# Loading a, q and k from SyncE's queue in single rows, in turn with crossbar transposes, in a fused linear-attention and MLP kernel

## Chip, cores, metric

One core of a Trainium2 chip. The metric is the device time in microseconds (us) of one execution; lower is better. Medians below are over all executions of a kernel.

## The reference

A gated linear recurrence per head, then a two-layer MLP with GELU on its output (shapes: 4 batches, 8 heads, 768 steps, head size 48; MLP 384 to 2048 to 384).

```python
for t in range(S):
    state = alpha[:, :, t, :, None] * state + np.einsum('bhd,bhe->bhde', k[:, :, t], v[:, :, t])
    y[:, :, t] = np.einsum('bhd,bhde->bhe', q[:, :, t], state)
# x = y as [3072, 384]
h = x @ w_in
g = 0.5 * h * (1.0 + np.tanh(c * (h + 0.044715 * h * h * h)))
return g @ w_out
```

## The kernel before

The steps are cut into 6 chunks of 128 and the batches into 2 halves, which gives 12 "pairs" (chunk, half). For each pair: load a (alpha), q, k, v; la = ln a; cum = running sum of la on TensorE; b = exp(cum), binv = exp(-cum), bend; q' = q b and k' = k binv (`qp`, `kp`); q' and k' transposed (`qkT`); scores `at` on TensorE; mask; `yps`; copied to x; x transposed (`xT`). Block m of the MLP is layer 1 (`hT`, GELU to `gT`) and layer 2 (`acc`) of pair m. A small planner in the kernel orders all instructions of all engines ahead of time, from planned costs `W`; engines then execute that order.

```python
DECAYS = {-1: (0, 1), 1: (2, 3), 2: (4,), 3: (5,), 4: (6, 7), 5: (8,), 6: (9,), 7: (10,), 8: (11,)}
TURN_QK, TURN_X = (8, 9, 10, 11), (8, 9, 10, 11)      # pairs transposed by the DMA crossbar
BUFS = dict(ca=1, yk=2, ff=4, la=3, qp=4, kp=4, b8=2, qkT=4, atm=6, x=3, ot=6, bend=8, a=4, q=4, k=4, v=6)
...
def load(self, n, c, i, lo=0, hi=2):
    def emit(e):
        ...
        src = self.src[n][2 * i + lo:2 * i + hi].rearrange("b h s d -> s (b h) d")[c * C:(c + 1) * C]
        (nc.sync if e == "SP" else nc.gpsimd).dma_start(u[n][:, lo:hi].rearrange("t b h d -> t (b h) d"), src)
...
def turn_dma(self, u, n):                               # crossbar transpose of q' or k'
    self.nc.sync.dma_start_transpose(self.qkT(u)[:, "qk".index(n)]..., u[n + "p"]...)
...
# GELUs of block m wait for the exponentials of DECAYS[m - 1];
# the logarithms of DECAYS[m] wait for the last GELU of block m
g = s.add("gelu", ..., [t] + between[m - 1] + ...)
ln.deps.append(gs[m][-1])
```

`DECAYS` sets the lead: the pairs in DECAYS[m] get their decays between the GELUs of blocks m and m + 1.

Of the kernel before, what the change touches and what calls it, by code (L numbers as in the profile page):

```python
# [5 lines left out]
BF16 = mybir.dt.bfloat16  # L6
F16 = mybir.dt.float16
F32 = mybir.dt.float32
# [3 lines left out]
LN_EXP, GELU = 6, 0  # L12


W = dict(
    ln=760, exp=720, bend=170, gelu4=510, gelu2=340, table=1290,
    cum=530, t8=450, t4=225, attn=340, kv=170, inter=170, intra=205, tx=168, l1_4=655, l1_2=340, l2=655,
    qk2=910, qk1=500, ev8=650, ev4=350, mask=640, st=1400, st0=700, xc=520, xe=330, ot=540,
    ev8_act=960, ev4_act=520, xc_act=450, xe_act=450, ot_act=450,
    strip=2120, cast=1500, weight=1850, dma=2100, issue=1100, wissue=760, sp=100, store=2600, turn=1250, landed=2200, xbar_qk=1500, xbar_x=1000, first=3470, cold=500, fill=216, zero=1100,  # L20
)
LAT = {"SP": 0, "PE": 210, "ACT": 110, "DVE": 90, "POOL": 0}

# [1 line left out]
class Task:  # L25


    def __init__(self, kind, cost, prio, emit, deps=(), table=None, land=None, stream=None, xbar=0, late=0):
        self.kind, self.cost, self.prio, self.emit = kind, cost, prio, emit
        self.deps, self.takes = list(deps), []  # L30
        self.table, self.land, self.stream, self.xbar = table, land, stream, xbar
        self.late = late
        self.end = self.done = None

    def take(self, tag, *users):
# [4 lines left out]
class Scheduler:  # L40
# [9 lines left out]
    def order(self):  # L50
        free = {e: 0 for e in LAT}
        taken = {tag: [] for tag in self.bufs}
        table, wire, xbar, head, out = LN_EXP, 0, 0, 0, []
        left = {e: sorted((t for t in self.tasks if e in t.cost), key=lambda t: t.prio) for e in LAT}

        def given(tag):

            n, at = len(taken[tag]) - self.bufs[tag], 0
            for u in taken[tag][n] if n >= 0 else ():
                if u.done is None:  # L60
                    return None
                at = max(at, u.done)
            return at

        def ready(t):
            if t.stream not in (None, head):
                return None
            at = 0
            for d in t.deps:
                if d.done is None:  # L70
                    return None
                at = max(at, d.done)
            for tag, _ in t.takes:
                g = given(tag)
                if g is None:
                    return None
                at = max(at, g)
            return at

        def put(t, at, e):  # L80
            nonlocal wire, xbar
            for tag, users in t.takes:
                taken[tag].append(users)
            t.start, t.end, t.engine, t.load = at, at + t.cost[e], e, None
            free[e] = t.end
            t.done = t.end + LAT[e]
            if t.land is not None:
                wire = t.done = max(wire, t.end + W["dma"] - t.land) + t.land
            if t.kind in ("turn", "store"):
                xbar = t.done = max(xbar, t.end + W["landed"] - t.xbar) + t.xbar  # L90
                t.done += t.late
            out.append(t)

        while any(left.values()):
            best = None
            for e in LAT:
                found = []
                for t in left[e]:
                    at = ready(t)
                    if at is not None:  # L100
                        turn = W["table"] if t.table not in (None, table) else 0
                        at = max(at, free[e] + turn)
                        found.append((at, t, at - turn))
                if found:
                    window = min(f[2] for f in found) + 60
                    at, t, _ = min((f for f in found if f[2] <= window), key=lambda f: (f[1].prio, f[0]))
                    if best is None or at < best[0]:
                        best = at, e, t
            assert best is not None, "no task can go on"
            at, e, t = best  # L110
            if e == "PE" and self.fill and at < self.until and at - free[e] > 500:
                g = given("ff")
                n = int((at - max(free[e], g if g is not None else at) - 100) * 0.8 // W["fill"])
                if not free[e]:
                    n = int((at - W["zero"]) // W["cold"])
                if n > 0:
                    f = Task("fill", {"PE": n * W["fill"]}, 0, self.fill(n))
                    put(f.take("ff", f), max(free[e], g), e)
            put(t, at, e)
            if t.stream is not None:  # L120
                head += 1
            if t.table not in (None, table):
                table = t.load = t.table
            for q in t.cost:
                left[q].remove(t)
        return out
# [9 lines left out]
class _Kernel:  # L136
# [6 lines left out]
    LOADS = ("0", "1", "in 0", "in 1", "in 2", "in 3", "out 0", "out 1", "out 2", "out 3",  # L143
             "2", "3", "4", "5", "6", "7", "8", "9", "10", "11")

    TURN_QK, TURN_X = (8, 9, 10, 11), (8, 9, 10, 11)
    BUFS = dict(ca=1, yk=2, ff=4, la=3, qp=4, kp=4, b8=2, qkT=4, atm=6, x=3, ot=6, bend=8,
                a=4, q=4, k=4, v=6)

# [63 lines left out]
    def load(self, n, c, i, lo=0, hi=2):  # L213

        nc, C, H, D = self.nc, self.C, self.H, self.D
        u = self.p[c, i]

        def emit(e):
            if n not in u:
                u[n] = self.tile(n, [C, 2, H, D], BF16 if n == "v" else F32)  # L220
            src = self.src[n][2 * i + lo:2 * i + hi].rearrange("b h s d -> s (b h) d")[c * C:(c + 1) * C]
            (nc.sync if e == "SP" else nc.gpsimd).dma_start(u[n][:, lo:hi].rearrange("t b h d -> t (b h) d"), src)  # L222
        return emit

    def load_w(self, which, part):
# [203 lines left out]
    def tasks(self):  # L429
        s = self.s = Scheduler(self.BUFS, self.fill, 60000)  # L430
# [3 lines left out]
        pairs = list(self.p)  # L434


        loads, n = {}, 0

        def load(key, cost, emit):
            nonlocal n  # L440
            land = W[{"v": "cast", "w": "weight"}.get(key[0], "strip")]
            loads[key] = s.add("load", {"POOL": cost}, n, emit, land=land // 2 if key[0] != "w" and key[1] in self.SPLIT else land)
            n += 1

        def rows(m, names="aqkv"):
            for lo, hi in self.parts(m):
                for r in names:
                    load((r, m, lo), W["issue"] * (hi - lo) // 2, self.load(r, *pairs[m], lo, hi))
                    loads[r, m, hi - 1] = loads[r, m, lo]
# [6 lines left out]
        for step in self.LOADS:  # L456
            if step == "0":
                rows(0, "qkv")
            elif step.isdigit():
                rows(int(step))  # L460
            else:
                weights(*step.split())


        states, ys, xts, lns, ends = {}, {}, {}, {}, {}
        for m, (c, i) in enumerate(pairs):
            u, P = self.p[c, i], 100 * m
# [3 lines left out]
            for lo, hi in self.parts(m):  # L471
                n = hi - lo
# [10 lines left out]
                step = 1 if early else n  # L483
# [7 lines left out]
            exps[0].take("b8", *qp, *kp)  # L491
            vs, kvs, tq, cs, users = [], [], [], [], []
            if m in self.TURN_QK:
                tq = [s.add("turn", {"SP": W["turn"]}, P + 10, self.turn_dma(u, n), d, xbar=W["xbar_qk"]) for n, d in (("q", qp), ("k", kp))]
                owner, turned = tq[0], tq
            for j in range(2):
                b, o = 2 * i + j, P + 10 + 3 * j
                k = kp[j]
# [18 lines left out]
                          ms + turned + [loads["v", m, j]] + ([states[b, c - 1]] if c else []))  # L517
                xc = s.add("x", {"ACT": W["xc_act"], "DVE": W["xc"]}, P + 20 + j, self.x(u, j), [y])
                if m in self.TURN_X:
                    xe = tx = s.add("turn", {"SP": W["turn"]}, P + 22 + j, self.turn_x_dma(u, j, c, b), [xc], xbar=W["xbar_x"])  # L520
                else:
                    tx = s.add("tx", {"PE": W["tx"]}, P + 22 + j, self.turn_x(u, j), [xc])
                    xe = s.add("xe", {"DVE": W["xe"]}, P + 22 + j, self.turned_x(u, j, c, b), [tx])
                    tx.take("yk", xe)
# [4 lines left out]
                xts[c, b], ys[b, c] = xe, y  # L529
                vs.append(y)  # L530
                if c < NCH - 1:
                    kv = s.add("kv", {"PE": W["kv"]}, P + 30 + j, self.kv(u, j), [k, loads["v", m, j]])
                    st = states[b, c] = s.add("st", {"DVE": W["st" if c else "st0"]}, P + 30 + j, self.carry(u, j, c, b),
                                              [kv, be[j]] + ([states[b, c - 1], ys[b, c - 1]] if c else []))
                    kv.take("yk", st)
                    vs.append(kv)
                    kvs.append(kv)
                    cs.append(st)
# [106 lines left out]
```

## Time and profile before

| | before |
|---|---|
| time, median | 188.67 us (188.61 to 188.9, 4 runs) |
| span in the profile, granted clock | 186.9 us, 1.00 |
| TensorE (PE) busy | 176.7 us, of which layer 1 69.9 and layer 2 68.6 |
| loads | all but one on GpSimd's queue (q0), 12 to 15 us from issue to landing |
| crossbar transposes of q', k' | pairs 8 to 11, 3.2 us to landing |

"Busy" is time in instructions; idle time in front of an instruction is given with what ended it. "Landing" is the moment when all data of a transfer have arrived. In the lines of the profile PE is TensorE and PEld its weight loads, DVE is VectorE, ACT ScalarE, POOL GpSimd, and SP or SPq SyncE. The prediction below shows the lines that carry the argument. In short: TensorE is full from 60 to 180 us, and DMA is full up to about 120 us but ahead of need.

### The profile page before, as it was taken

What the parts mean: (1) busy time and instruction counts of PE and PEld (TensorE: products, weight loads), DVE (VectorE), ACT (ScalarE), POOL (GpSimd) and SP (SyncE); (2) the same over time, 40 slices, a digit from 0 to 9 for tenths busy, and PEclk for the clock granted to TensorE, in tenths of its full rate; (3) what the DMA queues carried; (4) which work ended last, traced back from release to release, by engine and by line L of the source; (5) the groups of instructions that cost most, each with busy time, mean ns of one, the idle gap of its engine ahead of it and who ended that gap; (6) DMA issues with size and microseconds to landing.
All of it is one profiled execution on the core that took longest, in us unless ns stands there. A gap on an engine that the chain in (4) does not pass through costs nothing.

```text
span 186.9 us, 4504 instructions
## 1 busy us (share of the span) xinstructions
PE 176.7 (95%) x1831; PEld 127.2 (68%) x1834; DVE 104.0 (56%) x219; ACT 131.8 (71%) x297; POOL 63.8 (34%) x67
## 2 busy tenths in 40 slices
PE   5788899999999999999999999999999999999990
PEld 1344688666687687687688778667687687786850
DVE  7268670079787597497499798696644615000000
ACT  2544889853769769859799759788789884582911
POOL 7993443796456575566552200000000000000000
PEclk9999999999999999999999999999999999999999
DMA  6999999999999999999999997153270280301111
GB/s 131 174 183 169 206 204 212 200 178 229 240 217 186 151 227 205 175 231 200 180 218 222 186 207 136 43 123 76 46 178 22 49 190 14 101 15 47 42 42 44
DMA packets 49781, 27.56 MB, mean 147 GB/s; under 512 B 39744, under 2 KB 46400, under 8 KB 49760
## 3 DMA queue, kind: packets, MB, share of 16 engines
q0 software_dynamic: 32464, 19.27, 74.4%
q1 hardware_dynamic: 17296, 8.00, 17.5%
q8 instruction: 14, 0.23, 0.6%
q14 instruction: 7, 0.06, 0.1%
HBM read 25.17 MB, written 4.72 MB: 160 GB/s over the span
## 4 chain that ended last, share of the span: by engine, by line
PE 88%; ACT 4%; DVE 3%; DMA 2%; issue 1%
PE hT L400 34%; PE acc L414 34%; PE at L327 4%; PE qkT_ps L291 4%; PE cum L254 3%; PE yps L376 2%; DMA a<-in_alpha_dram 2%; PE yps L373 2%; PE kv L344 2%; PE idle L209 2%; PE xT_ps L390 1%; DVE atm L334 1%; ACT qkT L305 1%; PE cum L256 1%; DVE qp L280 1%
## 5 line engine op out<-in xcount | busy, mean ns | idle before, releaser
L406 ACT ACTIVATE gT<-hT 128x256 bf16<-128x256 f32 x192 | 63.5, 386 | 11.0 <-PE hT L400 10.5
L400 PE MATMUL hT<-xT,w_in 128*128 128x256 bf16 x576 | 69.9, 273 | 0.3 <-ACT gT L406 0.2
L414 PE MATMUL acc<-w_out,gT 128*128 128x384 bf16 x384 | 68.6, 326 | 0.0
L400 PEld LDWEIGHTS <-w_in 128*128 128x128 bf16 x576 | 54.2, 98 | 8.6 <-issue 0.8
L414 PEld LDWEIGHTS <-gT 128*128 128x128 bf16 x384 | 35.7, 97 | 20.4
L334 DVE TENSOR_TENSOR atm<-at,ut 128x512 bf16<-128x512 f32 x48 | 31.0, 686 | 13.8 <-PE at L327 12.9
L280 DVE TENSOR_TENSOR qp<-q,b 128x768 bf16<-128x768 f32 (+1 forms) x13 | 11.6, 892 | 19.0 <-ACT b L272 16.7
L421 ACT COPY ot<-acc 128x384 f32<-128x384 f32 x17 | 8.2, 480 | 18.7 <-PE acc L414 18.5
L222 POOL DMA_DIRECT2D k<-in_k_dram x13 | 14.5, 1113 | 12.3 <-DVE kp L280 6.0
L222 POOL DMA_DIRECT2D q<-in_q_dram x13 | 14.6, 1122 | 9.5 <-DMA q<-in_q_dram 3.0
L222 POOL DMA_DIRECT2D v<-in_v_dram x13 | 14.4, 1111 | 7.3 <-DMA a<-in_alpha_dram 2.7
L222 POOL DMA_DIRECT2D a<-in_alpha_dram x12 | 13.3, 1110 | 7.8 <-DMA k<-in_k_dram 1.9
L272 ACT ACTIVATE b<-cum 128x768 bf16<-128x768 f32 (+1 forms) x13 | 9.9, 762 | 7.7 <-PE cum L256 7.6
L243 ACT ACTIVATE la<-a 128x768 f16<-128x768 f32 (+1 forms) x13 | 10.2, 793 | 3.5 <-DMA a<-in_alpha_dram 3.3
L209 PE MATMUL idle<-zero 128*128 128x512 bf16 x31 | 11.2, 483 | 1.4 <-DVE zero L596 1.2
L361 DVE TENSOR_TENSOR st<-stmp,bend 64x192 bf16<-64x192 f32 x32 | 11.3, 353 | 1.7
L200 ACT ACT_TABLE_LOAD x9 | 11.5, 1283 | 0.9 <-PEq L629 0.7
L280 DVE TENSOR_TENSOR kp<-k,binv 128x768 bf16<-128x768 f32 (+1 forms) x15 | 11.7, 792 | 0.2 <-DMA k<-in_k_dram 0.2
L359 DVE TENSOR_TENSOR stmp<-kv,st 64x192 f32<-64x192 f32 x32 | 11.3, 352 | 0.9 <-PE kv L344 0.6
L406 ACT ACT_TABLE_LOAD x9 | 11.5, 1283 | 0.2
L305 DVE COPY qkT<-qkT_ps 128x1024 bf16<-128x1024 bf16 (+1 forms) x14 | 8.8, 649 | 4.7 <-PE qkT_ps L291 4.6
L383 DVE CAST x<-yps 128x384 bf16<-128x384 f32 x12 | 6.7, 556 | 7.6 <-PE yps L376 7.5
(43 smaller groups left out, 151.3 us busy)
## 6 DMA issues: line engine op xcount, KB each, us to landing
out_dram<-ot SPq DMA_DIRECT2D x24, 192.0 KB, 3.8
q<-in_q_dram POOLq DMA_DIRECT2D x11, 384.0 KB, 13.2
k<-in_k_dram POOLq DMA_DIRECT2D x11, 384.0 KB, 13.2
a<-in_alpha_dram POOLq DMA_DIRECT2D x10, 384.0 KB, 13.0
v<-in_v_dram POOLq DMA_DIRECT2D x11, 192.0 KB, 13.0
w_in<-in_moe_w_in_dram POOLq DMA_DIRECT2D x4, 384.0 KB, 11.8
w_out<-in_moe_w_out_dram POOLq DMA_DIRECT2D x4, 384.0 KB, 15.3
a<-in_alpha_dram SPq DMA_DIRECT2D x1, 384.0 KB, 4.2
```

Of the source, the lines that this page charges most:

```text
L200: nc.scalar.add_instruction(mybir.InstLoadActFuncSet(name=nc.get_next_instruction_name(), act_func_set_id=i, engine=mybir.EngineType.Activ ...
L209: self.nc.tensor.matmul(ps, self.zero[:, 0:self.C], self.zero, start=True, stop=True)
L222: (nc.sync if e == "SP" else nc.gpsimd).dma_start(u[n][:, lo:hi].rearrange("t b h d -> t (b h) d"), src)
L243: self.nc.scalar.activation(u["la"][:, lo:hi, :, 0:self.D], u["a"][:, lo:hi], AF.Ln)
L280: self.nc.vector.tensor_tensor(u[n + "p"][:, lo:hi, :, 0:self.D], u[n][:, lo:hi], u["b" if n == "q" else "binv"][:, lo:hi], op=ALU.mult)
L305: self.copy(e)(t, u.pop(("T_ps", i, which)))
L334: self.nc.vector.tensor_tensor(u["atm", i][:, o], u["at", i][:, o], self.ut[:, None, :].to_broadcast([self.C, self.H // 2, self.C]), op=AL ...
L359: nc.vector.tensor_tensor(s[ps], acc, old[ps, :, fs], op=ALU.add)
L361: nc.vector.tensor_tensor(new[ps, :, fs], acc, u["bend"][ps, i, :, None].to_broadcast([64, H // 2, D]), op=ALU.mult)
L400: self.nc.tensor.matmul(h, self.w_in[:, j, nt * self.C:(nt + 1) * self.C], self.xT[c][:, j, lo:hi].rearrange("p g t -> p (g t)"), start=j ...
L406: return lambda e: self.nc.scalar.activation(self.gT[c % self.NG][:, nt, lo * self.C:hi * self.C], f.pop(("h", c, lo, nt)), AF.Gelu_apprx_ ...
L414: self.nc.tensor.matmul(f["acc", c, b], self.gT[c % self.NG][:, nt, b * self.C:(b + 1) * self.C], self.w_out[:, nt, :], start=nt == 0, sto ...
```

## The change

The intent: take the transposes of q' and k' of three more pairs off the full TensorE. To make room on the DMA engines for the crossbar, a, q and k of pairs 4 to 11 leave GpSimd's queue for SyncE's, where a transpose can stand between two loads. (The DMA crossbar transposes a tile while it is moved; SyncE's loads move single rows of 48 float32 numbers, 192 bytes.) A gate keeps those loads from starting before k of pair 3 has landed. v stays on GpSimd, since it is cast to bf16 on the way. The planner now takes a row load to hold SyncE for 2.6 us.

```diff
-    strip=2120, ... sp=100, store=2600, turn=1250, landed=2200, xbar_qk=1500, xbar_x=1000, ...
+    strip=2120, ... sp=650, landed=2200, xbar_qk=1350, xbar_x=600, row=2600, ...
...
-            if t.kind in ("turn", "store"):
-                xbar = t.done = max(xbar, t.end + W["landed"] - t.xbar) + t.xbar
-                t.done += t.late
+            if e == "SP" and t.land is None:
+                t.done += W["landed"]
...
+    ON_SP = 4
-    TURN_QK, TURN_X = (8, 9, 10, 11), (8, 9, 10, 11)
+    TURN_QK, TURN_X = (5, 6, 7, 8, 9, 10, 11), (8, 9, 10, 11)
...
+    def hold(self, m, n, m1, n1):          # the gate: a copy on GpSimd that reads k of pair 3
+            self.nc.gpsimd.tensor_copy(u[n][:, 0, 0, 0:1], last[n1][:, 0, 0, 0:1])
...
+            if key[0] in "aqk" and key[1] >= self.ON_SP:
+                loads[key] = s.add("load", {"SP": W["row"]}, 100 * key[1] + 5, emit, [gate])
+                n += 1
+                return
...
-                    kv = s.add("kv", ..., [k, loads["v", m, j]])
+                    kv = s.add("kv", ..., [k, loads["v", m, j]] + ([states[b, c - 1], ys[b, c - 1]] if c else []))
```

## The prediction

> **What bounds the kernel now.** I read the page's first part first: TensorE (PE) is busy nearly all of the span, nothing else is near it.
>
> ```profile
> PE 176.7 (95%) x1831; PEld 127.2 (68%) x1834; DVE 104.0 (56%) x219; ACT 131.8 (71%) x297; POOL 63.8 (34%) x67
> ```
>
> A busy PE can still be a badly fed one, so next I read the table by stages of 10 us. Columns: stretch, busy time and instruction count of PE, PEld, DVE, ACT, POOL, then granted clock, DMA share, GB/s.
>
> ```profile
> 0.00:10.00 10.00, 6.90 (x28) 2.78 (x29) 4.64 (x23) 3.71 (x5) 8.77 (x15) 1.00 1.12 154
> 10.00:20.00 10.00, 8.18 (x93) 4.27 (x93) 8.37 (x18) 4.58 (x9) 6.57 (x9) 1.00 1.35 180
> ...
> 80.00:90.00 10.00, 10.00 (x121) 7.73 (x120) 7.27 (x17) 8.48 (x20) 5.77 (x6) 1.00 1.40 213
> 90.00:100.00 10.00, 10.00 (x124) 7.75 (x121) 8.23 (x15) 8.67 (x21) 5.76 (x5) 1.00 1.37 213
> ...
> 180.00:187.00 7.00, 2.72 (x17) 1.43 (x15) 0.00 (x0) 0.96 (x2) 0.00 (x0) 1.00 0.16 57
> ```
>
> PE is full from 60 us to 180 us but for 0.18 us. Of its 10.3 us of idle time, 4.9 lie in the first 20 us and 4.3 after its last matmul; neither is touched by the change. The list of waits of PE between 60 and 125 us is empty. So in the stretch that changes, the time is the sum of PE's instructions, and only two things can move it: fewer of them, or a new wait.
>
> At the same time the DMA engines are never idle up to about 120 us. The DMA view from 60 to 100 us shows who fills them; the shares are of packet time, overlapping, so they pass 100%.
>
> ```profile
> q0 software_dynamic: 15847, 6.79, 138.7%
> q1 hardware_dynamic: 862, 1.18, 11.7%
> ```
>
> GpSimd issues a load in 1.15 us and then waits about 0.95 us for an earlier one to land; 21 loads go out in these 40 us, one per 1.9 us. The loads are thus limited by DMA, but run ahead of their use: the last load of all is issued at 102.8 us, while the logarithm of the last pair's a starts only at 144.6 us. DMA is full, not binding.
>
> **What the Trainium skill says.** "TensorE: Matmul & The Clock Gate", section "Wait — 56ns, not 53.3ns?", gives 55.6 ns from start to start for back-to-back 128-column matmuls at the full clock. The trace agrees: sixteen transposes fill 0.89 us in the chain, 55.6 ns each (their listed 219 ns overlap), so that is what one costs.
> "DMA: Bandwidth & Descriptors", section "Queues, rings and completion order": each DMA engine drains one queue row's ring in order and takes turns between rows at packets. So a transpose behind three loads on SyncE's ring waits for them, while GpSimd's v loads only share. This trace has no such mix, so it neither confirms nor denies it.
> Same page, "Issuing engines are not separate DMA queues": issuing from another engine buys no bandwidth. The trace differs somewhat in favour of the change; the numbers are below.
>
> **The change part by part.**
> (1) PE. Pairs 5, 6 and 7 no longer transpose q' and k' on PE. The chain in order of time shows one such pair, start, length, what:
>
> ```profile
> 78.77 0.33 PE hT L400 x3
> 79.09 0.89 PE qkT_ps L291 x16
> 79.98 0.66 PE hT L400 x6
> ```
>
> It is on the path: layer 1 stands directly on both sides. 3 pairs x 16 x 55.6 ns = 2.67 us removed from a full engine. Check on the pairs that have it already: the second score block (at, L327) starts every 14.16 us for pairs 4 and 5 (68.57, 82.73), and 12.9 and 12.6 us apart (128.19, 141.10, 153.71) for the last three, which also lack other small PE work.
> (2) DVE. Six copies out of PSUM of 0.681 us go, 4.1 us. DVE is at 7 to 8 us in 10 here and off the path: worth nothing directly, but frees PSUM buffers earlier. The extra dependencies of kv only order the static schedule; no work is added.
> (3) GpSimd. 24 loads (8 pairs x a, q, k) of 1.12 us go, 27 us; one tiny copy as a gate comes, which waits for k of pair 3. Off the path.
> (4) SyncE. 24 loads, 6 more transposes. The one load that SyncE issues today took it 0.45 us; a transpose takes it 1.24 us. 24 x 0.45 + 6 x 1.24 = 18 us on a queue that is mostly waiting for stores.
> (5) DMA. What matters is how fast single 192-byte rows go. The DMA view of 1.5 to 3.5 us has SyncE's one load nearly by itself:
>
> ```profile
> GB/s 0 0 0 0 0 0 0 73 104 127 108 81 104 111 131 123 150 215 215 250 261 257 265 261 261 257 265 261 261 257 265 261 261 257 265 261 261 257 265 261
> ...
> q1 hardware_dynamic: 1826, 0.35, 86.3%
> ```
>
> 0.35 MB in 1826 packets is 192 bytes each, and after the ramp they run at 261 GB/s: 393 kB in 1.5 us, against 1.9 us per load for GpSimd's queue. The diff's own planning constant is 2.6 us (row=2600). The transposes: from 111 to 160 us SyncE's queue took 39.1% of 49 us, 19.2 us, for 4.28 MB; by bytes a q' or k' transpose (262 kB) is 1.2 us and a store (197 kB) 0.9 us (an estimate).
> DMA time needed per pair: 3 x 1.5 + v 1.9 + 2 x 1.2 + 2 x 0.9 = 10.6 us; with 2.6 us rows, 13.9 us. PE's pair will take 14.16 - 0.89 = 13.3 us. So it fits at the seen rate and just misses at the planned one.
> (6) The tightest place. Blocks 4 to 5 need both a of pair 6 and a of pair 7, whose logarithms run together from 88.2 us. The gate opens when k of pair 3 lands: issued 37.9, median 13.2 to landing, 51 us. To a of pair 7 there are 10 row loads, some 4 v, 2 transposes, 6 stores: 10 x 1.5 to 2.6 + 7.6 + 2.4 + 5.4 = 30 to 41 us, and 2 us to land. It comes at 83 to 94 us, when it is needed at about 87. At the measured rate there are 4 us to spare.
> Pair 4 itself: a lands at about 51 + 4.2 = 55.5 us, its logarithm starts at 59.9. In time.
> Sum: -2.67 us on the path, plus a share of the small waits. I expect about 0.5 us of new PE waits, where scores wait for a transpose that has to queue behind rows. 188.6 - 2.7 + 0.5 = 186.4 us.
>
> **The rivals.**
> Rival A, the transpose becomes the wait. Alone it lands in 3.2 us:
>
> ```profile
> qkT<-qp SPq DMA_TRANSPOSE x4, 3.2
> qkT<-kp SPq DMA_TRANSPOSE x4, 3.1
> ```
>
> Behind three row loads on the same ring it could take 3.2 + 4.5 = 7.7 us. PE executes in order, so a score block placed too early stalls it. For: the schedule is fixed ahead and counts 2.2 us to landing after SyncE's turn. Against: its plan lets every row load hold SyncE 2.6 us, longer than I expect, and it moves scores back between MoE matmuls, of which there are over 10 us per pair. If it happens in each of pairs 5 to 9 with 1 us, the gain is gone and 2 us are lost: 188 to 191 us.
> Rival B, loads late. SyncE takes its work in order, so a load stands behind a store or a transpose that waits for its input, even when its own buffer is free; and rows may run slower beside v and stores than alone. For: today's loads have a queue that never stops for compute. Against: four buffers each for a, q, k, and 40 us of lead at the end. If rows take 2.6 us or more, a of pair 7 is up to 7 us late, partly hidden by layer 2 of block 4 (5.2 us): 189 to 193 us.
> Rival C, the rest improves too. Freed DVE and PSUM time could remove the few PE waits past 20 us, 1.1 us in all: 185 us. This is close to a floor, as every remaining PE instruction stays; 2% would need 3.8 us, more than the 2.67 + 1.1.
> Rival D, it is hidden anyway: PE would then have been waiting for something else in those 0.89 us. The empty list of waits speaks against it; it would give 188.6.
>
> **Range and chances.** The clean case (some 60%) gives 185.6 to 187; A or D in a mild form (25%) 187 to 190; B or a strong A (12%) 190 and over; C a few per cent. Predicted 186.4 us, range 185.2 to 190.0. Faster by over 2% (below 184.85): 0.05. Within 2%: 0.85. Slower by over 2% (over 192.4): 0.10.
>
> **What would show it.** Right: transposes to PSUM (qkT_ps, L291 today) down from 128 to 80, PE busy 2 to 3 us less, PE full between 60 and 180 us, spacing of pairs 5 to 7 near 13.3 us, SyncE's loads at 1.5 to 2.2 us of DMA each. Rival A: PE or PEld of the scores waiting for the DMA of qkT, with landing over 6 us. Rival B: ACT waiting for a (or DVE for q, k) and a hole in PE around 85 to 105 us. Rival C: the first 60 us or the holes near 123 us shorter. The prediction is wrong if PE has more than 3 us of idle time between 60 and 180 us, or if PE's busy time hardly falls.

## The result

The changed kernel took 200.69 us (199.47 to 203.52, 4 runs) against 188.67 us: ratio 1.0613, 95% interval 1.0537 to 1.0689. It is slower by 6%. A ratio here is the mean time of one kernel's fast runs over that of the other's fast runs of the same rounds, so not quite the ratio of the medians.

The profiled execution was the slowest of the four (203.52 us) and counts as slow, being over 1.5% above the fastest. I therefore use it for where waits stand, and take sizes from experiments whose profiled runs were fast.

Its first part, then the granted clock by fortieths of the span, then the table by stages (columns as in the prediction):

```profile
PE 179.9 (89%) x1783; PEld 127.1 (63%) x1786; DVE 99.8 (50%) x212; ACT 132.4 (66%) x298; POOL 36.4 (18%) x44
...
PEclk9999999999999999995885999999999999999998
```

```profile
60.00:70.00 10.00, 7.02 (x73) 4.74 (x72) 4.72 (x9) 5.12 (x9) 1.14 (x1) 1.00 1.57 167
...
80.00:90.00 10.00, 8.13 (x72) 6.28 (x70) 5.11 (x11) 9.60 (x23) 0.00 (x0) 1.00 1.28 190
90.00:100.00 10.00, 8.13 (x60) 4.74 (x61) 3.93 (x7) 2.36 (x5) 0.00 (x0) 0.66 0.98 161
100.00:110.00 10.00, 6.95 (x82) 4.65 (x81) 8.49 (x18) 4.38 (x8) 1.14 (x1) 0.72 1.24 179
```

TensorE executes 48 instructions fewer (the transposes), yet is busy 3.2 us longer and idle 11 us longer. The holes are at 60 to 70 us and 80 to 110 us, and from 90 to 110 us the granted clock is 0.66 and 0.72: after the second hole the work that follows also runs slower. The timeline of TensorE shows the two first holes (start, length, instruction, count, and in brackets the idle time before it with its releaser):

```profile
68.11 0.40 PE L301 MATMUL qkT_ps<-ident,kp 128*128 128x128 bf16 x4 [2.98 <-DVE kp L290]
...
82.40 5.08 PE L410 MATMUL hT<-xT,w_in 128*128 128x256 bf16 x45
87.31 0.81 PE L424 MATMUL acc<-w_out,gT 128*128 128x384 bf16 x4
91.87 0.61 PE L337 MATMUL at<-qkT 64*128 64x128 bf16 x8 [3.74 <-DMA qkT<-kp]
92.41 4.02 PE L424 MATMUL acc<-w_out,gT 128*128 128x384 bf16 x12
```

First, k' of pair 4 comes 3 us late. Then TensorE runs 45 layer-1 matmuls in a row and four of layer 2, finds q' and k' of pair 5 not yet transposed, and waits 3.7 us for the crossbar. The twelve layer-2 matmuls after that take 4.02 us; before, twelve in one piece at 90.16 us took 2.11 us. That is the clock, 0.50 from 92.4 to 96.4 us. The Trainium skill, "TensorE: Matmul & The Clock Gate", section "HAM oscillation — how this bites in real kernels", gives the rule "no PE-idle gaps >~3.4µs". Here the gap is 3.74 us and the clock falls, while the single gap of 2.98 us at 65 us left it at 1.00. But it fell as well in a run whose longest gap there was 0.88 us (e3 below), so shorter gaps close together can do it too.

Why k' is late is seen on VectorE and on SyncE's queue (for a load, the length is how long SyncE was held in issuing it):

```profile
67.10 0.96 DVE L290 TENSOR_TENSOR kp<-k,binv 128x768 bf16<-128x768 f32 x1 [3.25 <-DMA k<-in_k_dram]
```

```profile
49.63 3.35 SPq L222 DMA_DIRECT2D q<-in_q_dram  x1
53.08 5.37 SPq L222 DMA_DIRECT2D k<-in_k_dram  x1
58.49 4.30 SPq L222 DMA_DIRECT2D a<-in_alpha_dram  x1
...
79.74 4.87 SPq L222 DMA_DIRECT2D q<-in_q_dram  x1
84.70 1.79 SPq L436 DMA_DIRECT2D out_dram<-ot  x1
86.59 1.32 SPq L320 DMA_TRANSPOSE qkT<-qp  x1
88.02 0.53 SPq L436 DMA_DIRECT2D out_dram<-ot  x1
88.60 1.29 SPq L320 DMA_TRANSPOSE qkT<-kp  x1
```

These row loads hold SyncE 3.4 to 5.4 us each, where I had counted 0.45 us of SyncE's time and 1.5 us of DMA time. The lower part is the second hole: k' of pair 5 was ready at 82.0 us (VectorE), but its transpose is issued at 88.6 us, because SyncE was first held 4.9 us by a load and then by two stores and the transpose of q'. Once issued, the transposes were not slow: the 14 of q' and k' took 3.0 to 4.9 us to landing, median 3.2 us, as before.

What slows the rows is in the DMA view of 53 to 58 us (packets, MB, share of packet time, overlapping):

```profile
q0 software_dynamic: 2561, 0.24, 89.6%
q1 hardware_dynamic: 2223, 0.42, 77.5%
```

GpSimd's queue now holds nothing but v. With no a, q, k between them, GpSimd has issued v of several pairs ahead at 39 to 46 us, and those packets (94 bytes each, since the cast halves the row) take more than every second turn. The rows get 0.42 MB in 5 us, 84 GB/s: 4.7 us per load.

The gate has a part in it. Before, GpSimd issued k of pair 4 at 42.5 us. Now its copy opens the gate at 49.1 us, and k goes out third, at 53.1 us. It then takes 13.9 us to landing, about what loads took before (median 13.2 us), so the late start alone makes up most of its delay. Without v it takes 6.5 us and comes in time behind the same gate (e3 below); without the gate it was not tried.

### The profile page after: what moved, and what is told of

It is laid out like the page before. It is cut to its first block, busy times and chain, and to the rows that moved or that the text cites. A ratio compares the mean times of both kernels' runs of the same rounds, so it can differ in the third digit from the quotient of the medians.

```text
span 201.3 us, 4402 instructions
## 1 busy us (share of the span) xinstructions
PE 179.9 (89%) x1783; PEld 127.1 (63%) x1786; DVE 99.8 (50%) x212; ACT 132.4 (66%) x298; POOL 36.4 (18%) x44
## 4 chain that ended last, share of the span: by engine, by line
PE 50%; DMA 29%; DVE 6%; POOL 6%; SPq 3%; ACT 2%; issue 2%; POOLq 0%; DVEq 0%
PE acc L424 23%; PE hT L410 17%; DMA w_out<-in_moe_w_out_dram 7%; DMA k<-in_k_dram 7%; DMA qkT<-kp 6%; DMA a<-in_alpha_dram 5%; DMA q<-in_q_dram 3%; PE at L337 3%; PE yps L383 2%; PE cum L264 2%; POOL w_in L240 1%; SPq L222 1%; DVE kp L290 1%; PE yps L386 1%; DVE atm L344 1%
## 5 line engine op out<-in xcount | busy, mean ns | idle before, releaser
L424 PE MATMUL acc<-w_out,gT 128*128 128x384 bf16 x384 | 70.2, 332 | 0.0
L410 PEld LDWEIGHTS <-w_in 128*128 128x128 bf16 x576 | 55.3, 99 | 9.8 <-issue 1.7
L424 PEld LDWEIGHTS <-gT 128*128 128x128 bf16 x384 | 36.2, 99 | 22.0 <-issue 1.9
L290 DVE TENSOR_TENSOR qp<-q,b 128x768 bf16<-128x768 f32 (+1 forms) x13 | 11.6, 891 | 17.0 <-ACT b L282 16.9
L337 PE MATMUL at<-qkT 64*128 64x128 bf16 x192 | 10.2, 229 | 6.7 <-DMA qkT<-kp 5.6
L337 PEld LDWEIGHTS <-qkT 64*128 64x128 bf16 x192 | 5.9, 98 | 13.0 <-DMA qkT<-kp 7.0
L393 ACT CAST x<-yps 128x384 bf16<-128x384 f32 x13 | 6.2, 479 | 10.4 <-PE yps L386 10.4
L209 PE MATMUL idle<-zero 128*128 128x512 bf16 x31 | 10.8, 469 | 1.4 <-DVE zero L612 1.2
L393 DVE CAST x<-yps 128x384 bf16<-128x384 f32 x11 | 6.1, 557 | 9.8 <-PE yps L386 9.8
L386 PE MATMUL yps<-v,atm 128*128 128x48 bf16 x192 | 9.2, 186 | 1.4 <-DVE atm L344 1.2
```

The lines of the kernel that those rows point to most:

```text
L290: self.nc.vector.tensor_tensor(u[n + "p"][:, lo:hi, :, 0:self.D], u[n][:, lo:hi], u["b" if n == "q" else "binv"][:, lo:hi], op=ALU.mult)
L337: nc.tensor.matmul(at[:, o, p, :], t[sl, 1, p, :], t[sl, 0, p, :], start=True, stop=True)
L386: nc.tensor.matmul(y[:, h, :], u["atm", i][:, h % 2, h // 2, :], u["v"][:, i, h, :], start=c == 0, stop=True, skip_group_check=True)
L393: self.copy(e)(x, u["y", i].rearrange("t h d -> t (h d)"))
L410: self.nc.tensor.matmul(h, self.w_in[:, j, nt * self.C:(nt + 1) * self.C], self.xT[c][:, j, lo:hi].rearrange("p g t -> p (g t)"), start=j ...
L424: self.nc.tensor.matmul(f["acc", c, b], self.gT[c % self.NG][:, nt, b * self.C:(b + 1) * self.C], self.w_out[:, nt, :], start=nt == 0, sto ...
```

## The experiments

Theories: **V**, v's packets take the DMA engines' turns from the rows; **L**, the crossbar's latency needs more lead than pairs 5 and 6 have; **H**, transposes stand behind rows and stores in SyncE's fixed order; **R**, single rows are slow in themselves; **X**, crossbar transposes under load are the harm. All results were correct except where said.

Most edits also make the planner order the engines anew, so a difference holds both the edit and its new order. Only leaving out v (e3 against the change, e11 against e8) keeps the planned order, since it replaces nothing but what a load emits.

| run | what | median us | ratio to before (95%) |
|---|---|---|---|
| e1 | rows only | 192.78 | 1.0209 (1.0166 to 1.0251) |
| e2 | crossbar for 7 pairs only | 233.71 | 1.2421 (1.2365 to 1.2477) |
| e3 | change, no v from pair 4 | 193.96 | 1.0293 (1.0243 to 1.0343) |
| e4 | change, 3 buffers for v | 196.75 | 1.0419 (1.0394 to 1.0444) |
| e5 | rows only, 3 buffers for v | 190.01 | 1.0073 (1.0057 to 1.009) |
| e6 | e5 and pair 7 on the crossbar | 189.96 | 1.0067 (1.0052 to 1.0082) |
| e7 | e4 and earlier decays | 191.85 | 1.0175 (1.0118 to 1.0232) |
| e8 | change, earlier decays | 200.39 | 1.0622 (1.0584 to 1.066) |
| e9 | change, v on SyncE | 201.9 | 1.0707 (1.0673 to 1.0741) |
| e10 | e9 and earlier decays | 200.92 | 1.0661 (1.0623 to 1.07) |
| e11 | e3 and earlier decays | 187.99 | 0.9964 (0.9938 to 0.9991) |
| e12 | before, earlier decays | 190.01 | 1.0069 (1.0047 to 1.0091) |
| e13 | e7, stores from GpSimd | 203.47 | 1.0781 (1.0729 to 1.0832) |
| e14 | e7, rows planned at 1.9 us | 201.72 | 1.0697 (1.0681 to 1.0713) |
| e15 | e2 and earlier decays | 218.88 | 1.1602 (1.1583 to 1.1621) |
| e16 | e13 and e14 | 212.28 | 1.1231 (1.1194 to 1.1267) |

### The two halves of the change by themselves

Rows only (e1): the changed kernel with

```diff
-    TURN_QK, TURN_X = (5, 6, 7, 8, 9, 10, 11), (8, 9, 10, 11)
+    TURN_QK, TURN_X = (8, 9, 10, 11), (8, 9, 10, 11)
```

> The loads part alone: a, q, k of pairs 4 to 11 on SyncE in single rows, q' and k' transposed on TensorE up to pair 7 as before. Theory V (GpSimd's v loads, now free to run ahead, take the DMA engines' packet turns from the rows, so k of pair 4 lands at 67 us instead of 56): still slow, 194 to 199 us, with the 3 us wait for k' of pair 4 near 65 us still there. Rival H (the harm is that transposes stand behind rows in SyncE's order): 188 to 190 us, since no transpose of pairs 5 to 7 is on SyncE.

192.78 us: below V's range and above H's. The late k' is there (2.17 us at 67.4 us, the only wait of TensorE over 0.4 us after 20 us in its profile). So the loads alone cost about 2%, and the rest of the 6% needs the transposes.

Crossbar only (e2): the kernel before with

```diff
-    TURN_QK, TURN_X = (8, 9, 10, 11), (8, 9, 10, 11)
+    TURN_QK, TURN_X = (5, 6, 7, 8, 9, 10, 11), (8, 9, 10, 11)
```

> The kernel before with only the list of pairs transposed by the crossbar widened to 5 to 11; all loads stay on GpSimd. Theory V: close to my sum, 185.5 to 188 us, as SyncE is free when q' is ready; at worst some waits because transposes share DMA engines with the load queue (4 to 6 us to landing instead of 3.2). Rival X (crossbar transposes under load are what stalls TensorE): 192 us or more, with scores waiting for the transposes of pairs 5 to 7.

233.71 us, far past even rival X. Scores wait 38.7 us for the crossbar. In the DMA view of 79 to 102 us, the first transposes take (us to landing):

```profile
qkT<-qp SPq DMA_TRANSPOSE x1, 14.6
qkT<-kp SPq DMA_TRANSPOSE x1, 25.3
```

against 3.2 us with the load queue empty, and all traffic falls to 113 GB/s in that stretch. My own sum (186.4 us) would have been wrong by 47 us on this kernel. This may also be why the change moves the loads at all: beside GpSimd's full load queue the wider use of the crossbar cost 45 us. In the changed kernel itself the transposes landed in 3.0 to 4.9 us, so X is not what slowed it.

e15 asks whether the lead was to blame there: e2 with

```diff
-    DECAYS = {... 2: (4,), 3: (5,), 4: (6, 7), 5: (8,), ...}
+    DECAYS = {... 2: (4, 5), 3: (6,), 4: (7,), 5: (8,), ...}
```

This moves the decays of pairs 5 and 6. Pair 7 had two blocks already and stays, although the expectations of e7 and e10 name it too.

> All loads on GpSimd, crossbar for pairs 5 to 11, earlier decays. If the short lead made the 233.7 us: under 200 us. If sharing the DMA engines with GpSimd's loads stretches a transpose to 15 to 25 us, as its trace shows: still over 215 us, since two blocks of lead are some 14 us more but the next pairs' transposes fall into loads as well.

218.88 us, 15 us better but still 16% above before, with waits of 10.1, 9.0 and 6.5 us for transposes. The sharing is the main part, as expected.

### Theory V: take v away, or hold it back

e3 replaces the v loads of pairs 4 to 11 by a constant (wrong result):

```diff
+            if n == "v" and 2 * c + i >= self.ON_SP:
+                self.nc.gpsimd.memset(u[n][:, lo:hi], 0.0625)
+                return
```

> The changed kernel with the v loads of pairs 4 to 11 replaced by a constant written by GpSimd (wrong result on purpose). Theory V: rows take 1.5 to 1.8 us each from 49 us on, k of pair 4 lands before 58 us, no wait near 65 us, 186 to 189 us. Rival R (single rows on SyncE are slow in themselves): rows of pairs 4 and 5 still 3.5 to 5 us each, 195 us or more. Rival H: rows fast but transposes of pair 5 still late, 190 to 195 us.

193.96 us: 6.7 us better than the change, but not the 186 to 189 of V alone; it falls into the range given to H. The DMA view of 49 to 58 us:

```profile
q1 hardware_dynamic: 8289, 1.75, 115.4%
q0 software_dynamic: 294, 0.03, 5.8%
```

The same row loads now move 1.75 MB in 9 us, 194 GB/s or 2.0 us per load in place of 4.7 us, and the wait near 65 us is gone. R falls. What stays is the hole at 85 to 100 us (below).

e4 keeps v and its result, but with fewer buffers GpSimd cannot run ahead:

```diff
-                a=4, q=4, k=4, v=6)
+                a=4, q=4, k=4, v=3)
```

> The changed kernel with 3 buffers for v in place of 6, so that GpSimd cannot load v of later pairs ahead of the rows of pair 4. Theory V: k of pair 4 lands near 60 us, wait near 65 us shorter than 1 us, 188 to 193 us. Rivals R and H: as the changed kernel, 198 to 202 us, or worse through later v.

196.75 us: 4 us better, less than I expected, though the wait near 65 us is gone. One number is cut by half and the time falls: v is a cause, and its being early accounts for 3.9 of the 6.7 us that leaving it out gains. e5, the same in the rows-only kernel:

> Rows on SyncE alone (q' and k' of pairs 5 to 7 on TensorE again) and 3 buffers for v. Theory V: the wait for k' of pair 4 near 65 us goes and with it the loss of the rows: 188 to 190 us, against 192.8 with 6 buffers. If rows are slow for another reason: 191 us or more.

190.01 us against 192.78: at the upper end of the range. Rows on SyncE, with v held back, cost 0.7%.

### Theory L: lead

In e3 the two transposes of pair 5 are issued 0.1 and 1.2 us after their data are ready (78.1 and 79.0 us), and still the timeline of TensorE has a hole:

```profile
89.58 0.33 PE L403 MATMUL xT_ps<-ident,x 128*128 128x128 bf16 x3
...
92.73 0.40 PE L340 MATMUL at<-qkT 64*128 64x128 bf16 x8 [0.66 <-ACT bend L281]
...
96.19 0.50 PE L403 MATMUL xT_ps<-ident,x 128*128 128x128 bf16 x3
97.57 1.44 PE L413 MATMUL hT<-xT,w_in 128*128 128x256 bf16 x6 [0.88 <-DVE xT L407]
```

The last line is block 5's first layer 1: it waits for x of pair 5, whose second half was transposed at 96.2 us; in the kernel before both halves were at 87.3 and 88.2 us. With the crossbar the first scores of pair 5 come at 85.1 us instead of 80.6. By then the running sums of pairs 6 and 7 are due, which share the one `ca` buffer with scores, and the second scores stand behind both (released by `bend`, the last reader of that buffer). This chain is read from the trace; what was tested is the lead, with the `DECAYS` edit of e15. The granted clock between 95 and 100 us is 0.53 here, though no gap of TensorE is longer than 0.88 us: between 90 and 95 us it is busy only 3.0 of 5 us, in small pieces (columns as in the prediction).

```profile
90.00:95.00 5.00, 3.02 (x39) 1.95 (x37) 4.21 (x9) 1.58 (x3) 0.00 (x0) 1.00 0.76 155
95.00:100.00 5.00, 3.91 (x41) 2.55 (x42) 4.28 (x10) 2.53 (x4) 0.74 (x1) 0.53 0.83 150
```

e6 stays with e5 and adds only pair 7, which has the longer lead already (TURN_QK from 7):

> As the run before, with pair 7 on the crossbar too. Theory L (the crossbar costs some 6 us of latency, and pairs 5 and 6 have their decays only one block ahead of their use while pairs from 7 on have two): pair 7 has the lead, so 0.9 us of TensorE is saved and no hole appears between 85 and 100 us: 187.5 to 189.5 us. If any more crossbar work beside rows stalls TensorE: 191 us or more.

189.96 us, half a microsecond over the range, but with no hole at 85 to 100 us, as L says. The 0.9 us saved on TensorE does not show in the time. Scores wait 2.4 us for the crossbar in 4 places, against 1.7 us in 2 in e5, and TensorE is busy 176.2 us against 175.8. (With all 128 transposes on TensorE, in the kernel before, e1, e5 and e12, it is busy 175.8 to 176.7 us, so a saving of this size can be lost in the spread.) e7 is e4 with the earlier decays:

> The changed kernel with 3 buffers for v and with the decays (logarithm, exponentials) of pairs 5, 6 and 7 moved one block earlier, so that every crossbar pair has two blocks of lead. Theory V + L: both causes gone, the hole between 85 and 100 us gone, the granted clock 1.00 throughout: 185.5 to 189 us. If L is wrong: as with 3 buffers alone, 195 to 197 us, with the hole still there.

191.85 us: 4.9 us gained over e4 by moving the decays, though 2.9 us above the range. The hole is gone: TensorE is busy 14.97 of the 15 us from 85 to 100. e8 has the decays without the buffers:

> The changed kernel with the earlier decays alone, 6 buffers for v. Theory V + L: the late k of pair 4 stays (2 to 3 us, near 65 us) and a of pair 5, now needed some 14 us earlier, comes late as well: 190 to 198 us, slower than the run before by 3 us or more. If V is wrong: equal to it within 1 us.

200.39 us, above the range of 190 to 198. No gain at all, because pair 5's a is now needed before v lets it through (the waits of ScalarE for a: in all, times, longest; the longest is pair 5's, and in e7 the same wait is 1.6 us):

```profile
ACT la L253 <- DMA a<-in_alpha_dram: 16.3, 5, 10.5
```

The lead alone gains nothing, fewer buffers for v alone 3.9 us, both together 8.8 us: V and L are both needed. e11 takes out both (no v, earlier decays; wrong result):

> No v loads from pair 4 on (wrong result on purpose) and the earlier decays. Theory L: the whole difference to the run without v alone (194.0) is the hole of pair 5, so about 5 us less: 187 to 190 us, no idle stretch of TensorE over 1 us between 60 and 130 us. If the hole comes from something else: 193 to 195 us.

187.99 us, inside the range, 0.4% under the kernel before. Its profile and the stage that had the hole:

```profile
PE 174.2 (94%) x1786; PEld 124.3 (67%) x1786; DVE 100.8 (54%) x214; ACT 131.3 (71%) x296; POOL 32.9 (18%) x44
```

```profile
80.00:100.00 20.00, 19.97 (x230) 15.53 (x229) 14.78 (x31) 16.74 (x41) 0.74 (x1) 1.00 1.11 188
```

TensorE is busy 2.5 us less than before, and full in this stretch. This is the saving that I had predicted, in a kernel that does not load its v. Only 0.7 us of it reaches the time: TensorE is idle 1.4 us longer than before, and scores wait 1.8 us for the crossbar. The control e12, the earlier decays in the kernel before:

> Control: the kernel before with the earlier decays alone. They take nothing from TensorE, so the same within 0.5%: 188 to 189.5 us. If they gain by themselves (over 1 us), the gain of the lead in the changed kernel is not only that of the crossbar's latency.

190.01 us, 0.5 us over the range, so the decays gain nothing by themselves; they lose 0.7%.

### What keeps the repaired kernel above the kernel before: theory H

e9 removes the second queue by bringing v on SyncE as f32, cast by GpSimd; e10 adds the earlier decays:

```diff
+            if key[0] == "v" and key[1] >= self.ON_SP:
+                f = s.add("load", {"SP": W["row"]}, 100 * key[1] + 5, self.load("vf", *pairs[key[1]]), [gate])
+                loads[key] = s.add("cast", {"POOL": 1300}, n, self.cast_v(*pairs[key[1]]), [f])
...
-    row=2600
+    row=1750
```

> The changed kernel with v of pairs 4 to 11 brought by SyncE too, in rows of f32 behind its a, q and k, and cast to bf16 by GpSimd (1.3 us planned each); the planner counts 1.75 us for a row load, as measured without v beside it. Theory V: with one queue nothing overtakes, rows take 1.6 to 2.2 us, no wait for k' near 65 us; the hole of pair 5 (theory L) stays: 191 to 195 us, like the run without v. If rows beside v were not the cause: 198 us or more.

> The run before with the decays of pairs 5, 6, 7 one block earlier as well. Theory V + L: both causes gone, result correct: 186 to 190 us, and if waits for transposes behind rows stay under 2 us in all, a little below the kernel before. Rival H (transposes in SyncE's order wait behind rows and stores whatever the lead): 190 to 193 us, like the run with 3 buffers for v and the lead, with 3 to 5 us of scores waiting for the DMA of qkT.

201.9 and 200.92 us: both expectations missed, and e9 lies where I had put the case that rows beside v are not the cause. The trace speaks against that case: the part of V holds (rows hold SyncE 1.6 to 3.1 us, no wait for k' near 65 us), but scores wait 10.3 and 9.9 us for the crossbar. SyncE now has four rows per pair as well as transposes and stores in one order: in e9, k' of pair 5 is ready at 79.6 us and its transpose is issued at 85.7, behind a load, two stores and the transpose of q'. What v on SyncE costs by itself stays open: both runs also plan a row at 1.75 us instead of 2.6 and give v's float32 rows only two buffers, and e14 below shows that a shorter planned row alone can cost 10 us.

Two more runs on e7: stores moved to GpSimd (e13), and only the planned cost of a row changed (e14); e16 has both.

```diff
-  s.add("store", {"SP": W["sp"]}, ...)      # and nc.sync.dma_start
+  s.add("store", {"POOL": 1100}, ...)       # and nc.gpsimd.dma_start          (e13, e16)
-  row=2600
+  row=1900                                  #                                  (e14, e16)
```

> 3 buffers for v, earlier decays, and the output stores issued by GpSimd instead of SyncE. Rival H in the form 'stores in SyncE's order hold up transposes': 188 to 190 us, waits of scores for qkT under 2.5 us in all instead of 5.1. If the stores are not what holds them up: 191 to 193 us.

> 3 buffers for v, earlier decays, and the planner counting 1.9 us per row load instead of 2.6 (only the static order changes). If a wrong plan is what is left: 188.5 to 190.5 us. If not: 191 to 193 us.

> e13 and e14 in one: 3 buffers for v, earlier decays, stores from GpSimd, 1.9 us per row in the plan. A candidate to beat the kernel before: 187 to 189.5 us if both remaining waits are gone; 190 us or more if v beside rows still delays the transposes.

203.47, 201.72 and 212.28 us: all three far worse, the opposite of what I expected. Waits of scores for the crossbar are 11.2, 11.6 and 16.8 us against 5.1 in e7. e14 shows why, as only the static order differs. First e7, k' of pair 5 on VectorE and its transpose on SyncE; then e14:

```profile
73.93 0.96 DVE L290 TENSOR_TENSOR kp<-k,binv 128x768 bf16<-128x768 f32 x1
```

```profile
74.92 1.23 SPq L320 DMA_TRANSPOSE qkT<-kp  x1
```

```profile
74.27 0.96 DVE L290 TENSOR_TENSOR kp<-k,binv 128x768 bf16<-128x768 f32 x1
```

```profile
75.79 0.53 SPq L222 DMA_DIRECT2D q<-in_q_dram  x1
76.42 2.52 SPq L222 DMA_DIRECT2D k<-in_k_dram  x1
78.98 3.53 SPq L222 DMA_DIRECT2D a<-in_alpha_dram  x1
82.61 2.54 SPq L320 DMA_TRANSPOSE qkT<-kp  x1
```

In e7 the transpose goes out as soon as k' is done. In e14 the planner, believing in shorter rows, has put three loads before it, which hold SyncE for 6.8 us; the scores then wait 6.5 us. So H is real, and the planned 2.6 us per row, longer than 21 of the 24 rows hold SyncE in e7, is what left gaps in which transposes could go out. For e13 and e16 the cause stays open: taking the stores away packs SyncE's order more tightly too, but stores from GpSimd also share its queue with v, and I did not separate these.

No version with correct results was faster than the kernel before; the best changed ones are e6 and e5, 0.7% slower.

## Why the prediction was wrong, point by point

The saving was right; a cost, a wait and a place were wrong. By its own sign the prediction failed too: it allowed 3 us of idle TensorE between 60 and 180 us, and the profiled run has 12.0 us.

- **TensorE's saving** was right: 80 transposes instead of 128, and 174.2 us busy against 176.7 in e11, where little else is in the way. The predicted 2.67 us was there to be had.
- **Step (4), SyncE's time, failed.** I took 0.45 us per row load from the one load that SyncE issued on an empty queue, 10.8 us for 24. In the profiled run the 24 row loads hold SyncE for 46.7 us (46.0 us in e8, whose profiled run was fast), and still 33.5 us without v (e3). So SyncE was not a queue "mostly waiting for stores", and transposes came late because they could not be issued.
- **Step (5), the DMA time, failed with it.** I took 1.5 us per row load from a stretch in which SyncE's load was alone, and added v as one more term of a sum. Beside v a row load took 4.7 us; without v 2.0 us, no better than the 1.9 us of GpSimd's queue, so the advantage that I had read from the lone load was not there. The terms were added as if they took turns load by load, as in one queue; in two queues they take turns packet by packet, and the one with nothing between its loads is served ahead of need. I had quoted the page that says so and used it only for transposes.
- **Step (6), the tightest place, was the wrong place.** I checked a of pair 7 (it came in time) and of pair 4 (in time), but not k of pair 4, third on the new queue. I had the gate's opening nearly right (51 us, really 49), but not that k would land 18 us after it; k' waited 3.25 us for it.
- **Rival A was named and sized wrongly.** I had a transpose wait in the ring, behind rows, for up to 7.7 us to landing; it landed in 3.0 to 4.9 us and waited before its issue instead. I gave the rival 1 us per pair on the ground that the planner moves scores back between MLP matmuls, "of which there are over 10 us per pair". It did move them back, behind all of layer 1 of block 4, and that made x late for block 5. Moving the decays is worth 4.9 us (e4 to e7) and 6.0 us (e3 to e11) where v is out of the way.
- **Rival B** had the right start (SyncE's order holds things up, rows slower beside v) and a range of 189 to 193 us. It took loads as the victims; the transposes behind loads were hit too.
- **The clock was left out.** In the profiled run TensorE is busy 5.7 us longer than in e11 with the same instructions but three records (179.9 to 174.2), at a mean clock of 0.963. In this run idle time was paid about one and a half times: some 11 us of new idle and 5.7 us of slow running. The three fast runs had clocks of 0.974 to 0.991 and lost less.

Adding up, as one path among several since the parts are not independent: e11 would stand at 186.0 (188.7 - 2.7) if the crossbar were free and stands at 188.0, so 2.0 us of small waits; the short lead adds 6.0 (to e3, 194.0), v adds 6.7 (to 200.7). The gate stands in all of these runs.

## What to carry to other kernels

Before moving transfers to a second queue, ask what the first queue will do once they are gone: what stays behind may run ahead and take the engines from transfers that are needed sooner. Replacing an operation on a full engine by one with more latency needs lead for everything that hangs on it, so look up when its consumer's consumer is due, not only whether the engine has other work. And in a queue that is served in order, planned slack before an urgent item can be worth more than a correct duration: planning rows shorter cost 10 us in e14.

## What the Trainium skill lacked or had wrong

- "DMA: Bandwidth & Descriptors", section "Queues, rings and completion order", says that an engine takes turns between queue rows by packets. The runs agree, and give the consequence that it does not: beside v the row queue got 2223 of 4784 packets and a 393 kB load took 4.7 us, without it 2.0 us.
- The same page, section "DMA Transpose (X-bar)", warns of two transposing streams, and its rules say that a transpose next to ordinary DMAs needs nothing. That is about correctness and held (e2 was correct), but no page that I read gives the time of a transpose beside other traffic: beside GpSimd's full load queue those of q' and k' took 14.6 and 25.3 us to landing against 3.2 us, and 233.7 us against 188.7 in all.
- "Perfetto Trace Analysis", section "DMA Instruction — HWDGE (DVE, Sync)", has the issuing sequencer free for its next instruction only when all descriptors of a transfer are made. It gives no time for it, and no page that I read says how it grows with what is still queued: a row load held SyncE 0.45 us with an empty queue and 3.4 to 5.4 us beside v, so that a transpose behind it could not even be issued.
- "TensorE: Matmul & The Clock Gate", section "HAM oscillation — how this bites in real kernels": its rule of gaps over 3.4 us is not the whole of it. The page's next section, "A second HAM failure mode: psum-queue depth-cycling", does tell of short idles that make the clock swing, but gives no length. In e3 the mean clock was 0.53 from 95 to 100 us, after 5 us in which TensorE was busy 60% with no gap over 0.88 us.
- No page that I read gives the packets of a casting load: v went in packets of 94 bytes on average, so at half the bytes it takes as many turns as an uncast row load.
